# Clearing a value tile in eight pieces, and spreading one-hot tiles over more half pairs, in a chunked attention and top-1 mixture-of-experts kernel

## The chip, the cores and the metric

The kernel runs on one core of a Trainium2 chip. The metric is the device time of one execution in microseconds (us). The kernel before takes 444.6 us, the median of three runs (444.13, 444.6, 446.34).

## What is computed

Attention over chunks of 32 queries, each of which sees 8 memory rows, its own chunk, 16 rows to the left and 8 to the right; then, on the rows of all heads side by side, a mixture of 8 experts in which each token goes to the one with the largest logit.

```
for c in range(nc):                       # B, H, S, D = 4, 8, 768, 64; chunks of 32
    l_start, r_end = max(0, 32*c - 16), min(S, 32*c + 40)
    k_full = concat([mem_k, k[:, :, l_start:r_end]]); v_full likewise
    a = softmax(scale * q_c @ k_full.T)
    out[:, :, c_start:c_end] = a @ v_full
x = out as [3072, 512]
logits = x @ w_gate + modality_bias[modality_id]
e_idx = argmax(logits); gate_w = softmax(logits)[e_idx]
out[mask_e] = gate_w * (relu(x[mask_e] @ w1[e]) @ w2[e])   # 8 experts, 512 -> 1024 -> 512
```

## The kernel before

The kernel has two stages. The first does the attention and, beside it, the routing of the tokens. The second gathers the tokens of each expert from a copy of x in memory and does the two matrix products.

**The attention loop** (`for i in range(n + 2)`, line 894) goes over 16 pairs of heads, `u`, each in two half pairs, `hf`, so 32 steps `i`. Four pairs make a batch. It is a software pipeline written out by hand: TensorE (PE), SyncE (SP) and GpSimd (POOL) keep the order of the program throughout (line 50), VectorE (DVE) and ScalarE (ACT) keep it up to step 26 (`MAN`). In step `i` PE gets, in this order: `scores` of this half pair (line 351); `exps_t` of the one before, a transpose of the scores less their maximum (line 369), from which ACT makes the exponentials `PT` (line 371); in a first half (`hf == 0`) the transposes of the next pair's keys (`trans_k`, lines 333 and 337), which ACT copies into the tile `kbd` in four copies (`store_k`, line 343), and in a second half the transposes of the next pair's queries (`trans_q`, line 315), copied by ACT to `qT` (line 320); `trans_x` of the half pair two steps back (line 404); and `attend` of the one before, the weighted sum of values (line 381). DVE has, in a step, the maximum and the subtraction (`less_max`, lines 359 and 362), in a first half the regrouping of the next pair's queries to `qr` (line 306), and `normalize` of the half pair before (`den`, its reciprocal, and the product `xb`, lines 389, 391, 396). POOL shares the value rows between chunks (`share_v`, line 301, eight copies for a pair), writes the memory keys of the pair after the next into `kbd` (`mem_keys`, line 325) and issues the store of `xb` (line 409). PSUM tiles of the name `tr` (`bank()`) come from four buffers that all these transposes share.

**The value tiles.** There are three, `vws[0]` to `vws[2]`, used in turn by the pairs. Each holds two heads beside each other with zeros across, and the zeros are written once, ahead of a tile's first use: those of the third tile by two DVE memsets of 64 partitions x 24 x 64, one after `normalize` of step 1 (line 952) and one after `less_max` of step 2 (line 907). Pair 2 first needs the tile in step 5.

**The routing** of batch `b` is a generator, `route(b)` (line 536), appended when the batch's last attention rows are transposed. It yields "v" after each DVE or POOL instruction and "pe" or "late" ahead of work for PE. `pump(k)` (line 414), called all over the loop with k = 1, 3 or 5, takes up to k instructions from it. A wait for PE is taken up only by the last `pump(1, True)` of a step, behind `attend`, and only so many steps after the yield: for batches 0 and 1 one step after "pe" and two after "late", for batch 2 none and one. The parts that the change touches are, for batches 0 and 1: the logits reach DVE (line 553), DVE finds the largest (`oh`, line 572), ACT takes exponentials (`rex`, line 575), `yield "pe"` (line 576), PE forms the ranks by products with `ones_b` and `tri_b` (lines 581 to 586), DVE goes on with gate, rank, `lo` and `ac` (lines 589 to 615), then six pairs of one-hot tiles, `l1` (128 x 128, line 654) and `a1` (128 x 192, line 656), two pairs by POOL and four by DVE, then `yield "late"` and the six table products on PE (line 664).

```
def pump(k, pe=False):
    ...
        if wait:
            if not pe or now[0] < since + (wait == "late" or b < B - 2) + (wait == "late" and b < B - 2):
                return
...
eng = nc.gpsimd if t < (NPOOL, NPOOL, NPOOL, NP3)[b] else nc.vector
```

Constants for the routing (`more_constants`, line 194) are made by DVE in the same way from step 4 on.

Of the kernel before, what the change touches and what calls it, by code (L numbers as in the profile page):

```python
# [20 lines left out]
P = 128  # L21
B, H, S, D = 4, 8, 768, 64
NMEM = 8
NCH = S // 32
NT = S // P
# [28 lines left out]
def tile_chunk_attention_top1_moe(  # L54
# [14 lines left out]
    nc = tc.nc  # L69
# [24 lines left out]
    def bank():  # L94
        return ps.tile([P, 512], F32, name="tr", tag="tr", bufs=4)
# [33 lines left out]
    vws = [(sv if i == 1 else pers).tile([P, NCH, VW], F32, name=f"vw{i}", align_bytes=256) for i in range(NVW)]  # L129
# [140 lines left out]
    def edge_v(i):  # L270
        t = vws[i]
        for h in range(2):
            r = slice(64 * h, 64 * h + 64)
            nc.gpsimd.memset(t[r, :, 2 * D:2 * D + 2], 0.0)
            nc.gpsimd.memset(t[r, 1:NCH - 1, 2 * D + h:2 * D + h + 1], 1.0)
            nc.gpsimd.memset(t[r, 0:NCH:NCH - 1, h * D:h * D + D], 0.0)
            nc.gpsimd.tensor_copy(t[r, 0:NCH:NCH - 1, 2 * D + h:2 * D + h + 1], vedge[r])
# [61 lines left out]
    def store_k(u, h, j, copy):  # L339
        tt = kts[u, h][64 * j:64 * j + 64]  # L340
        win = bass.AP(tensor=tt.tensor, offset=tt.offset, ap=[list(tt.ap[0]), [16, NCH], [1, 28]])
        dst = kbds[u % 2][64 * h:64 * h + 64, :, h, 0:56]
        copy(dst.rearrange("p c (i j) -> p c i j", j=2)[:, :, :, j], win)  # L343
# [12 lines left out]
    def less_max(u, hf):  # L356
        scf = scs.pop((u, hf))[:, 0:384].rearrange("p (a m) -> p a m", m=64)
        mx = sm.tile([P, 6, 1], F32, name="mx")
        nc.vector.reduce_max(mx, scf, axis=AX.X)
        pump(1)  # L360
        sb = sbs[u, hf] = wk.tile([P, 6, 64], F32, name="sb")
        nc.vector.tensor_sub(sb, scf, mx.to_broadcast([P, 6, 64]))
# [49 lines left out]
    routing, now = [], [0]  # L412

    def pump(k, pe=False):
        k = 1 if routing and routing[0][2] < 0 else k * KB if routing and routing[0][2] == B - 2 else k
        while k > 0 and routing:
            g, wait, b, since = routing[0]
            if wait:
                if not pe or now[0] < since + (wait == "late" or b < B - 2) + (wait == "late" and b < B - 2):
                    return  # L420
                pe = False
            r = next(g, None)
            if r is None:
                routing.pop(0)
                return
            routing[0] = (g, r if r != "v" else "", b, now[0])
            k -= r == "v"


    plan = {}  # L430
# [105 lines left out]
    def route(b):  # L536
# [36 lines left out]
        yield "v"  # L573
        ex = sm.tile(sh, F32, name="rex")
        nc.scalar.activation(ex, l, AF.Exp)
        yield "pe"

        rkb = bank()
        rkf = rkb[:, 0:(NT + 1) * E]
# [60 lines left out]
        for t in range(NT):  # L640
            l1 = rt.tile([P, P], F32R, name="l1", bufs=NT)
            a1 = rt.tile([P, 192], F32R, name="a1", bufs=NT)
            T = b * NT + t
            if b == B - 1 and NP3 <= t < NP3 + NACT:
                dist = sm.tile([P, 192], F32, name="dist", bufs=2)
                nc.scalar.activation(dist[:, 0:P], iota[:, 0:P], AF.Abs, scale=-1.0, bias=lo[:, t])
                nc.scalar.activation(l1, dist[:, 0:P], AF.Relu, scale=-1.0, bias=1.0)
                dist = sm.tile([P, 192], F32, name="dist", bufs=2)
                nc.scalar.activation(dist, iota, AF.Abs, scale=-1.0, bias=ac[:, t])
                nc.scalar.activation(a1, dist, AF.Relu, scale=tokn[:, T:T + 1], bias=tokm[:, T:T + 1])  # L650
                hot.append((l1, a1))
                continue
            eng = nc.gpsimd if t < (NPOOL, NPOOL, NPOOL, NP3)[b] else nc.vector
            eng.tensor_scalar(l1, iota[:, 0:P], lo[:, t], None, op0=ALU.is_equal)
            yield "v"
            eng.tensor_scalar(a1, iota, ac[:, t], tokm[:, T:T + 1], op0=ALU.is_equal, op1=ALU.mult)
            yield "v"
            hot.append((l1, a1))
        if b == B - 1:
            plan_early()  # L660
# [210 lines left out]
    t = bank()  # L871
# [3 lines left out]
    mem_keys(0, nc.gpsimd)  # L875
    nc.gpsimd.memset(vws[1][64:P, :, 0:D], 0.0)
    edge_v(1)
    for h in (1, 0):
        for j in range(2):
            store_k(0, h, j, nc.vector.tensor_copy if j else nc.scalar.copy)  # L880
# [13 lines left out]
    for i in range(n + 2):  # L894
# [8 lines left out]
            exps_t(*units[i - 1])  # L903
        if live:
            less_max(u, hf)
            if i in (1, 2):
                nc.vector.memset(vws[i][0:64, :, D:2 * D], 0.0)
            pump(1)
        if u + 1 < NU and hf == 0:
            trans_k(u + 1)  # L910
# [37 lines left out]
            trans_x(*units[i - 2])  # L948
        if 1 <= i < n:
            normalize(*units[i - 1])  # L950
            if i == 1:
                nc.vector.memset(vws[2][64:P, :, 0:D], 0.0)
            pump(1)
        if i >= 2:
            u2, hf2 = units[i - 2]
            if hf2 == 1 and u2 % 4 == 3:
                routing.append((route(u2 // 4), True, u2 // 4, 0))
# [197 lines left out]
```

## Time and profile before

| | before |
|---|---|
| median of three runs | 444.6 us |
| the profiled execution | 441.84 us |
| its span, first to last instruction | 440.1 us |
| mean granted TensorE clock | 0.989 of full |
| busy: PE, DVE, ACT, POOL | 415.1, 309.8, 268.6, 208.2 us |

The attention loop takes about the first 138 us, the experts the rest. The profile is of one execution, which is 2.8 us under the median of the runs. A share of busy time over the span mixes the two stages, so the views by stretch and the timelines are what to read; PE's busy time holds the modelled ends of pipelined matmuls and is no proof that PE sets the pace.

### The profile page before, as it was taken

How to read it: one execution, taken by the hardware profiler on the slowest of the kernel's cores; microseconds unless marked ns; L12 is line 12 of the kernel's file. 1: busy time of each engine (PE TensorE's matmuls, PEld its weight loads, DVE VectorE, ACT ScalarE, POOL GpSimd, SP SyncE). 2: the span in 40 equal slices, each digit the busy share in tenths (PEclk: the TensorE clock that was granted, in tenths of full speed). 3: DMA queues.
4: the chain of work that ended last, by engine and by line, in shares of the span. 5: the costliest groups of instructions: out<-in, count | busy, mean ns of one | idle time of the engine just before them, and what ended most of it. 6: DMA issues, size and time to landing. Idle time of an engine off the chain costs nothing. (4 is left out here: it accounts for less than half of the span.)

```text
span 440.1 us, 11873 instructions
## 1 busy us (share of the span) xinstructions
PE 415.1 (94%) x4053; PEld 355.7 (81%) x4053; DVE 309.8 (70%) x754; ACT 268.6 (61%) x537; POOL 208.2 (47%) x407
## 2 busy tenths in 40 slices
PE   7799998999987998999999999999999999999993
PEld 4677777777765886989798998989898989898982
DVE  6898797697796999658456466776768684959530
ACT  5868786787656664647365456666666565657521
POOL 7898889999687932550053305404041215220101
PEclk9999998999998999999999999999999999999998
DMA  6969998888566301296195967505596404350101
GB/s 191 234 167 249 219 262 239 231 231 228 131 185 221 138 8 48 97 259 208 38 281 170 243 182 262 170 32 161 124 250 206 140 5 148 99 144 1 48 1 48
DMA packets 78307, 69.31 MB, mean 158 GB/s; under 512 B 36763, under 2 KB 64563, under 8 KB 78228
## 3 DMA queue, kind: packets, MB, share of 16 engines
q1 hardware_dynamic: 71488, 48.84, 40.2%
q0 software_dynamic: 5888, 19.41, 14.8%
q8 instruction: 37, 0.61, 0.6%
q14 instruction: 42, 0.34, 0.2%
q10 hardware_dynamic: 852, 0.11, 0.2%
HBM read 81.25 MB, written 16.58 MB: 222 GB/s over the span
## 5 line engine op out<-in xcount | busy, mean ns | idle before, releaser
L803 PEld LDWEIGHTS tr<-xt,w 128*128 128x128 f32 x1152 | 140.8, 188 | 5.2 <-issue 2.8
L803 PE MATMUL tr<-xt,w 128*128 128x256 f32 (+1 forms) x1152 | 142.8, 284 | 2.1 <-PEq L1116 0.8
L813 PE MATMUL av<-wh,h 128*128 128x512 f32 x384 | 125.0, 397 | 0.0
L807 DVE SCALAR_TENSOR_TENSOR h<-tr,h 128x256 fp32r<-128x256 f32 x96 | 40.5, 423 | 66.8 <-ACT h L804 42.6
L813 PEld LDWEIGHTS av<-wh,h 128*128 128x128 f32 x384 | 72.1, 188 | 16.6 <-issue 0.4
L813 PE MATMUL av<-wl,h 128*128 128x512 f32 x192 | 75.6, 394 | 0.0
L301 POOL COPY vw<-vw 24x384 f32<-24x384 f32 (+1 forms) x128 | 67.2, 525 | 9.4 <-DMA vw<-in_v_dram 3.1
L804 ACT ACTIVATE h<-tr 128x256 fp32r<-128x256 f32 x96 | 36.9, 386 | 54.4 <-PE tr L803 40.7
L728 DVE TENSOR_TENSOR wl<-raw,wh 128x512 fp32r<-128x512 f32 x91 | 64.4, 708 | 7.0 <-ACT wh L726 0.5
L838 POOL DMA_INDIRECT out_dram<-o,ix x24 | 24.7, 1027 | 93.5 <-ACT o L834 90.7
L728 DVE TENSOR_TENSOR w<-raw,w 128x512 fp32r<-128x512 f32 x93 | 60.8, 693 | 5.9 <-ACT w L726 5.9
L726 ACT CAST wh<-raw 128x512 fp32r<-128x512 f32 x96 | 58.8, 616 | 0.0
L726 ACT CAST w<-raw 128x512 fp32r<-128x512 f32 x96 | 52.9, 623 | 0.0
L343 ACT COPY kbd<-tr 64x672 f32<-64x672 f32 x62 | 48.3, 778 | 5.4 <-DMA raw<-in_moe_modality_id_dram 2.2
L813 PEld LDWEIGHTS av<-wl,h 128*128 128x128 f32 x192 | 36.1, 188 | 7.6
L834 ACT ACTIVATE o<-av,gate 128x512 f32<-128x512 f32 x24 | 16.2, 689 | 39.2 <-PE av L813 27.3
L746 POOL DMA_INDIRECT xg<-xd,gx x24 | 26.7, 1111 | 17.0 <-POOL gx L744 5.5
L371 ACT ACTIVATE PT<-tr 128x384 f32<-128x384 f32 x32 | 15.8, 494 | 26.3 <-PE tr L369 26.1
L381 PE MATMUL av<-vw,PT 128*32 128x130 f32 x768 | 28.8, 284 | 2.7 <-ACT PT L371 2.7
L351 PE MATMUL sc<-kbd,qT 128*32 128x128 f32 x768 | 28.3, 279 | 1.3 <-DVE kbd L343 1.3
L381 PEld LDWEIGHTS av<-vw,PT 128*32 128x32 f32 x768 | 19.8, 111 | 8.2 <-issue 4.1
L351 PEld LDWEIGHTS sc<-kbd,qT 128*32 128x32 f32 x768 | 21.0, 112 | 5.0 <-issue 3.5
(251 smaller groups left out, 515.2 us busy)
## 6 DMA issues: line engine op xcount, KB each, us to landing
raw<-in_moe_w_dram SPq DMA_DIRECT2D x192, 256.0 KB
k<-in_k_dram SPq DMA_DIRECT2D x16, 384.0 KB
q<-in_q_dram SPq DMA_DIRECT2D x16, 384.0 KB
xd<-xb POOLq DMA_DIRECT2D x16, 384.0 KB, 4.8
vw<-in_v_dram SPq DMA_DIRECT2D x32, 184.0 KB
xs<-xg SPq DMA_DIRECT2D x14, 256.0 KB
xq<-xs SPq DMA_DIRECT2D x28, 128.0 KB
vw<-in_mem_v_dram SPq DMA_DIRECT2D x32, 48.0 KB
```

Source lines behind the costliest of these rows:

```text
L301: nc.gpsimd.tensor_copy(vw[r0:r0 + 24, c + 1:c + 1 + w, d], vw[r0 + 32:r0 + 56, c:c + w, d])
L343: copy(dst.rearrange("p c (i j) -> p c i j", j=2)[:, :, :, j], win)
L351: nc.tensor.matmul(sc[32 * j:32 * j + 32, t * P:(t + 1) * P], qT[:, 32 * c:32 * c + 32], kbd[:, c].rearrange("p h m -> p (h m)"), start=Tr ...
L381: nc.tensor.matmul(avb[32 * j:32 * j + 32, t * W:(t + 1) * W], PT[:, t * P + 32 * j:t * P + 32 * j + 32], vw[:, c, 0:W], start=True, stop= ...
L726: nc.scalar.copy(wh[i], raw[i])
L728: (eng or nc.vector).tensor_sub(wl[i][:, s], raw[i][:, s], wh[i][:, s].bitcast(F32))
L746: nc.gpsimd.indirect_dma_start(out=xg[t], out_offset=None, in_=xd[0:rows], in_offset=bass.IndirectOffsetOnAxis(ap=gx[:, t:t + 1], axis=0))
L803: nc.tensor.matmul(pw, wt[i][:, j * P:(j + 1) * P], x[:, c, 0:w], start=(n == 0), stop=(n == 11))
L804: nc.scalar.activation(hh[:, f], ph, AF.Relu)
L807: nc.vector.scalar_tensor_tensor(hl[:, f], ph, 0.0, hh[:, f].bitcast(F32), op0=ALU.max, op1=ALU.subtract)
L813: nc.tensor.matmul(pos[t], x, w[8 + f], start=(f == 0 and n == 0), stop=(f == 7 and n == 2))
L838: nc.gpsimd.indirect_dma_start(out=out, out_offset=bass.IndirectOffsetOnAxis(ap=to[:, t:t + 1], axis=0), in_=outs[t], in_offset=None, boun ...
```

## The change

It does two things. The two large memsets of the third value tile become eight of 64 partitions x 6 x 64 (`clear_v`): three after `normalize` of step 2, three after that of step 3, two after `less_max` of step 4. And the routing of batches 0 and 1 is paced in another way: the rank products wait for nothing but the last `pump(1, True)` of the same step ("now"); a DVE one-hot instruction yields "h", which counts 3 where k is 3 and 1.6 elsewhere, and is not begun with less than 1.5 left, so that a step gets fewer of them; the table products wait one step after the last tile in place of two.

```diff
--- before.py
+++ after.py
@@ -413,10 +413,14 @@
 
     def pump(k, pe=False):
         k = 1 if routing and routing[0][2] < 0 else k * KB if routing and routing[0][2] == B - 2 else k
+        heavy = 3 if k == 3 else 1.6
         while k > 0 and routing:
             g, wait, b, since = routing[0]
-            if wait:
-                if not pe or now[0] < since + (wait == "late" or b < B - 2) + (wait == "late" and b < B - 2):
+            if wait == "h":
+                if k < 1.5:
+                    return
+            elif wait:
+                if not pe or now[0] < since + (wait == "late" or wait != "now" and b < B - 2):
                     return
                 pe = False
             r = next(g, None)
@@ -424,7 +428,7 @@
                 routing.pop(0)
                 return
             routing[0] = (g, r if r != "v" else "", b, now[0])
-            k -= r == "v"
+            k -= heavy if r == "h" else r == "v"
 
 
     plan = {}
@@ -573,7 +577,7 @@
         yield "v"
         ex = sm.tile(sh, F32, name="rex")
         nc.scalar.activation(ex, l, AF.Exp)
-        yield "pe"
+        yield "now" if b < B - 2 else "pe"
 
         rkb = bank()
         rkf = rkb[:, 0:(NT + 1) * E]
@@ -651,10 +655,11 @@
                 hot.append((l1, a1))
                 continue
             eng = nc.gpsimd if t < (NPOOL, NPOOL, NPOOL, NP3)[b] else nc.vector
+            slow = "h" if b < B - 2 and eng is nc.vector else "v"
             eng.tensor_scalar(l1, iota[:, 0:P], lo[:, t], None, op0=ALU.is_equal)
-            yield "v"
+            yield slow
             eng.tensor_scalar(a1, iota, ac[:, t], tokm[:, T:T + 1], op0=ALU.is_equal, op1=ALU.mult)
-            yield "v"
+            yield slow if t < NT - 1 else "v"
             hot.append((l1, a1))
         if b == B - 1:
             plan_early()
@@ -875,6 +880,12 @@
     mem_keys(0, nc.gpsimd)
     nc.gpsimd.memset(vws[1][64:P, :, 0:D], 0.0)
     edge_v(1)
+    clears = [vws[2][64 * h:64 * h + 64, c:c + 6, (1 - h) * D:(2 - h) * D] for c in range(0, NCH, 6) for h in range(2)]
+
+    def clear_v(k):
+        for _ in range(k):
+            nc.vector.memset(clears.pop(0), 0.0)
+
     for h in (1, 0):
         for j in range(2):
             store_k(0, h, j, nc.vector.tensor_copy if j else nc.scalar.copy)
@@ -903,8 +914,10 @@
             exps_t(*units[i - 1])
         if live:
             less_max(u, hf)
-            if i in (1, 2):
-                nc.vector.memset(vws[i][0:64, :, D:2 * D], 0.0)
+            if i == 1:
+                nc.vector.memset(vws[1][0:64, :, D:2 * D], 0.0)
+            if i == 4:
+                clear_v(2)
             pump(1)
         if u + 1 < NU and hf == 0:
             trans_k(u + 1)
@@ -948,8 +961,8 @@
             trans_x(*units[i - 2])
         if 1 <= i < n:
             normalize(*units[i - 1])
-            if i == 1:
-                nc.vector.memset(vws[2][64:P, :, 0:D], 0.0)
+            if i in (2, 3):
+                clear_v(3)
             pump(1)
         if i >= 2:
             u2, hf2 = units[i - 2]
```

How that moves the instructions is shown at three places.

**DVE at step 4, ahead of pair 3's queries.** `vw_128` is the third value tile, `q_281` the queries of pair 3, `iota`, `rev`, `base` and `ones_b` are constants. Before:

```order
L396 TENSOR_TENSOR xb<-av,den 128x384
L195 CAST iota<-raw 128x192
L674 COPY base<-iota 64x8
L359 TENSOR_REDUCE mx<-sc 128x6
L197 TENSOR_SCALAR rev<-iota 128x8
L362 TENSOR_TENSOR sb<-sc,mx 128x384
L199 MEMSET ones_b 128x128
L306 COPY qr<-q_281 128x2x6x64
```

Now:

```order
L396 TENSOR_TENSOR xb<-av,den 128x384
L887 MEMSET vw_128 64x6x64 x3
L195 CAST iota<-raw 128x192
L359 TENSOR_REDUCE mx<-sc 128x6
L197 TENSOR_SCALAR rev<-iota 128x8
L679 COPY base<-iota 64x8
L362 TENSOR_TENSOR sb<-sc,mx 128x384
L887 MEMSET vw_128 64x6x64 x2
L199 MEMSET ones_b 128x128
L306 COPY qr<-q_281 128x2x6x64
```

Three pieces stand behind the `xb` of step 3 and two more ahead of the `qr` of pair 3; three others stand behind the `xb` of step 2. The two large memsets stood ahead of the `qr` of pair 2, earlier than this piece.

**PE where batch 0's ranks are formed.** The piece begins in the second half of pair 5; `kbd_124` belongs to pair 6. Before:

```order
L404 MATMUL tr<-ident,xb 128x128 x3
L381 MATMUL av<-vw_128,PT 32x130 x12
L351 MATMUL sc<-kbd_124,qT 32x128 x12
L369 MATMUL tr<-ident,sb 128x128 x3
L333 MATMUL tr<-ident,k_919 128x128 x3
L337 MATMUL tr<-ident,mkp 128x2x8
L333 MATMUL tr<-ident,k_919 128x128 x3
L337 MATMUL tr<-ident,mkp 128x2x8
L404 MATMUL tr<-ident,xb 128x128 x3
L381 MATMUL av<-vw_128,PT 32x130 x12
L581 LDWEIGHTS ones_b
L581 MATMUL tr<-tot,ones_b 128x56
```

Now, to where the rank products begin (the scores of pair 6 follow behind the last of them, with `tri_b`):

```order
L315 MATMUL tr<-ident,qr 128x128 x6
L404 MATMUL tr<-ident,xb 128x128 x3
L381 MATMUL av<-vw_128,PT 32x130 x12
L585 LDWEIGHTS ones_b
L585 MATMUL tr<-tot,ones_b 128x56
L587 LDWEIGHTS ones_b
L587 MATMUL tr<-oh,ones_b 128x48
```

The rank products stood behind the weighted sum of the following first half; they now stand behind that of the second half, ahead of pair 6's scores. Batch 1 moves in the same way. The table products keep their place behind the same weighted sum as before.

**DVE at batch 0's one-hot tiles.** Before, from `less_max` of a first half:

```order
L362 TENSOR_TENSOR sb<-sc,mx 128x384
L306 COPY qr<-q_1079 128x2x6x64
L654 TENSOR_SCALAR l_1389<-iota,lo 128x128
L656 TENSOR_SCALAR a_1390<-iota,ac,tokm 128x192
L654 TENSOR_SCALAR l_1393<-iota,lo 128x128
L656 TENSOR_SCALAR a_1394<-iota,ac,tokm 128x192
L654 TENSOR_SCALAR l_1401<-iota,lo 128x128
L656 TENSOR_SCALAR a_1402<-iota,ac,tokm 128x192
L389 TENSOR_SCALAR den<-av 128x6
L654 TENSOR_SCALAR l_1426<-iota,lo 128x128
L391 RECIPROCAL den<-den 128x6
L656 TENSOR_SCALAR a_1427<-iota,ac,tokm 128x192
```

Now, from `less_max` of the second half ahead of it:

```order
L362 TENSOR_TENSOR sb<-sc,mx 128x384
L659 TENSOR_SCALAR l_1315<-iota,lo 128x128
L661 TENSOR_SCALAR a_1316<-iota,ac,tokm 128x192
L659 TENSOR_SCALAR l_1340<-iota,lo 128x128
L661 TENSOR_SCALAR a_1341<-iota,ac,tokm 128x192
L389 TENSOR_SCALAR den<-av 128x6
L391 RECIPROCAL den<-den 128x6
L396 TENSOR_TENSOR xb<-av,den 128x384
L359 TENSOR_REDUCE mx<-sc 128x6
L362 TENSOR_TENSOR sb<-sc,mx 128x384
L306 COPY qr<-q_1085 128x2x6x64
L659 TENSOR_SCALAR l_1403<-iota,lo 128x128
```

All eight instructions stood ahead of the next `xb`; now four stand ahead of it, two behind the next `qr`, and the last two in the half pair after. On DVE `oh` itself keeps its place. On POOL the gate's store and the four one-hot instructions of each of the two batches now stand ahead of one more `share_v` and `mem_keys`.

## Rows read from the trace of the kernel before

**Rows 1.** Stretches: start:end, length, PE, PEld, DVE, ACT, POOL busy, clock, DMA share, GB/s
```profile
20.00:30.00 10.00, 8.18 (x142) 6.46 (x135) 9.06 (x27) 7.59 (x14) 9.21 (x16) 1.00 0.78 197
...
60.00:70.00 10.00, 8.37 (x155) 6.85 (x158) 8.82 (x27) 6.71 (x13) 9.07 (x15) 0.92 0.92 243
```

**Rows 2.** The chain that ended last, earliest long piece: start, length, what
```profile
364.63 11.67 PE tr L803 x96
```

**Rows 3.** Timeline of PE, pairs 3 to 5: start, length, line, count, idle before
```profile
31.14 0.86 PE L351 MATMUL sc<-kbd,qT 128*32 128x128 f32 x24
...
38.13 0.86 PE L351 MATMUL sc<-kbd,qT 128*32 128x128 f32 x24
...
43.30 0.87 PE L315 MATMUL tr<-ident,qr 128*128 128x128 f32 x6 [0.24 <-ACT kbd L343]
```

**Rows 4.** Timeline of DVE, 3 to 30 us: clears, and the copy of q
```profile
3.07 1.34 DVE L135 MEMSET vw<- 64x1536 f32 x1 [0.27 <-issue]
...
4.68 1.34 DVE L136 MEMSET kbd<- 64x1536 f32 x1 [0.27 <-issue]
...
27.29 0.50 DVE L306 COPY qr<-q 128x768 f32<-128x768 f32 x1
...
29.23 0.55 DVE L396 TENSOR_TENSOR xb<-av,den 128x384 f32<-128x384 f32 x1
```

**Rows 5.** Timeline of PE, 22 to 30 us
```profile
22.15 0.84 PE L315 MATMUL tr<-ident,qr 128*128 128x128 f32 x6 [1.49 <-DVE den L389]
...
29.92 0.52 PE L404 MATMUL tr<-ident,xb 128*128 128x128 f32 x3
```

**Rows 6.** Timeline of POOL, 30 us
```profile
30.34 0.74 POOL L325 COPY kbd<-memT 64x192 f32<-64x192 f32 x2
```

**Rows 7.** Timeline of PE around the routing of batch 0
```profile
53.00 0.87 PE L381 MATMUL av<-vw,PT 128*32 128x130 f32 x24
...
53.69 0.84 PE L351 MATMUL sc<-kbd,qT 128*32 128x128 f32 x24
...
57.58 0.20 PE L581 MATMUL tr<-tot,ones_b 128*128 128x56 bf16 x1
...
57.88 0.86 PE L351 MATMUL sc<-kbd,qT 128*32 128x128 f32 x24
...
68.12 0.58 PE L404 MATMUL tr<-ident,xb 128*128 128x128 f32 x3 [1.40 <-DVE xb L396]
...
68.62 1.53 PE L381 MATMUL av<-vw,PT 128*32 128x130 f32 x24
...
69.92 1.51 PE L351 MATMUL sc<-kbd,qT 128*32 128x128 f32 x24
...
79.27 0.84 PE L351 MATMUL sc<-kbd,qT 128*32 128x128 f32 x24
```

**Rows 8.** Timeline of DVE around the routing of batch 0
```profile
55.08 0.15 DVE L389 TENSOR_SCALAR den<-av 128x6 f32<-128x6 f32 x1
...
55.20 0.29 DVE L572 TENSOR_TENSOR oh<-rev,me 128x48 bf16<-128x48 f32 x1
...
67.42 0.55 DVE L396 TENSOR_TENSOR xb<-av,den 128x384 f32<-128x384 f32 x1
```

**Rows 9.** Timeline of PE around the routing of batch 1
```profile
86.59 0.84 PE L351 MATMUL sc<-kbd,qT 128*32 128x128 f32 x24
...
101.21 0.86 PE L351 MATMUL sc<-kbd,qT 128*32 128x128 f32 x24
...
109.69 0.84 PE L351 MATMUL sc<-kbd,qT 128*32 128x128 f32 x24
```

**Rows 10.** Timeline of DVE at the routing of batch 1
```profile
87.43 0.21 DVE L572 TENSOR_TENSOR oh<-rev,me 128x48 bf16<-128x48 f32 x1
```

**Rows 11.** Timeline of POOL from batch 0's one-hot tiles to pair 9's memory keys
```profile
66.90 0.75 POOL L654 TENSOR_SCALAR l<-iota,lo 128x128 fp32r<-128x128 f32 x1
...
74.83 0.74 POOL L325 COPY kbd<-memT 64x192 f32<-64x192 f32 x2
```

## The prediction

> **What bounds the kernel now.** I read the stretches of ten us first. They show where engines run short: from 20 to 30 us and from 60 to 70 us DVE and POOL are each busy for about nine us of ten, and in the second stretch the granted clock of TensorE is 0.92, in the first 1.00 [rows 1]. The chain of waits comes next; its first long piece begins at 364.63 us, so it says nothing of the attention loop [rows 2]. What the loop loses is carried whole to the experts, since their first products wait for the routing; I count a loss or gain in the loop one to one in the end. So the timelines of the loop decide.
>
> Undisturbed, a pair takes 6.99 us from scores to scores (31.14 to 38.13 us), and the query transposes in its second half stand behind ACT's key copies (the 0.24 us wait at 43.30 us) [rows 3]. That is a loop through two engines: query transposes, transposes of half pair outputs, weighted sum, scores and transposed scores on PE; exponentials and four key copies on ACT; query transposes again. What PE waits for between the query transposes of a second half and the next scores is lost in full; in a first half, behind the key transposes, PE has time to spare while ACT copies. Three places stand out. At 22.15 us PE has waited 1.49 us: the queries' copy stood behind the second memset of the third value tile [rows 5]. At 68.12 us it has waited 1.40 us for an `xb` that DVE began at 67.42, behind eight one-hot instructions, and after that the clock was low: the weighted sum took 1.53 us where 0.87 is usual, the scores 1.51 where 0.84 is [rows 7, 8]. Batch 1 has the same instructions and no such wait: from the scores of pair 10 to those of pair 13 it is 109.69 - 86.59 = 23.10 us [rows 9], where batch 0, pair 6 to pair 9, takes 79.27 - 53.69 = 25.58 [rows 7]. So 2.48 us is what batch 0's crowd of one-hot tiles costs.
>
> **Term 1, the memsets.** Two memsets in a row start 1.61 us apart (3.07 and 4.68), though each row shows 1.34 [rows 4]. So the two of the third tile cost 3.2 us. A piece is a quarter: 0.40 us if the 0.27 us gap belongs to the work, 1.34 / 4 + 0.27 = 0.61 if each instruction pays it. I take 0.43, near the first, as a gap that is the same in front of a kbd and a vw tile of one size looks like work that the row leaves out; eight pieces make 3.4 us (3.2 to 4.9). The wait at 22.15 us goes, but nothing is kept of it: POOL's memory keys for pair 3, which the change leaves alone, end at 30.34 + 0.74 = 31.08 [rows 6], and pair 3's scores already start at 31.14 [rows 3]. So the gain is at most 0.06. The other way is open. All eight pieces still stand ahead of pair 3's `qr`, DVE does the same work plus 0.2 us, and it now comes early to weighted sums that are not there yet, where a memset filled the time before. I put that idling at 0.3 us (between 0 and the 1.49 us by which PE's old wait moves). `qr` (27.29) and the `xb` at 29.23 move back by 0.5 us, PE's transposes at 29.92 follow that `xb` at once [rows 4, 5], and so does everything behind. Term 1: +0.5 us, from -0.06 to 1.7 + 0.3 = +2.0.
>
> [...]
>
> **Term 2, batch 0.** What goes: the crowd, 2.48 us. What comes: the rank products now stand directly behind a second half's weighted sum, at 53.69 us in the trace's time, ahead of pair 6's scores, and all but the first read `oh`. DVE's order up to `oh` is unchanged, and there `oh` runs from 55.20 to 55.49 [rows 8]. PE waits, then needs about 0.3 us for the products (57.58 to 57.88 where they stood) [rows 7]; pair 6's scores start at 55.82 and not 53.69, 2.13 us later. They stand in the part of the loop where nothing hides a wait; their old place, in a first half, cost little. Behind this DVE has caught up, and the one-hot instructions are four, two and two. I replay: 55.82, a pair of 6.99, 0.25 for an `xb` that comes late behind `lo` and `ac` (an estimate, below the 1.40 us of the old wait), a pair of 6.99, and for the pair with the table products and the next logits 109.69 - 101.21 = 8.48 [rows 9]. Pair 9's scores start at 78.53, before at 79.27. Term 2: -0.7 us. Its ends: -2.5 if `oh` were there in time, +1.4 if the 2.13 us came and the crowd's cost stayed but for the slow clock (0.66 + 0.67 us by the two long rows).
>
> **Term 3, batch 1.** Here PE is at the place at 86.59 us [rows 9] and `oh` ends at 87.64 [rows 10]; with 0.05 us to be seen by PE and the products' 0.3, pair 10's scores come 1.4 us later. Two pairs of 6.99 and one of 8.48 then make 1.4 + 22.46 = 23.86 us against 23.10. Term 3: +0.8 us, from 0 (`oh` in time) to +1.4.
>
> **What costs nothing.** The table products do not move on PE, so neither does the next batch's start. On POOL the gate's store and one-hot tiles go ahead of one `share_v` and `mem_keys` more. From the first one-hot to the end of the memory keys behind a `share_v` POOL needs 74.83 + 0.74 - 66.90 = 8.67 us [rows 11]; it can start when `ac` and `lo` are there, some 5 us after `oh` (estimate), at 60.5, and end at 69.2. Pair 8's scores, which need those keys, are due at 53.69 + 2.13 + 14.23 = 70.05. That covers it by 0.9 us; without the cover it is a wait on the critical loop.
>
> **Sum:** 0.5 - 0.7 + 0.8 = +0.6 us. The profiled execution, 441.84 us with a span of 440.1, would become 442.4; it lies 2.8 us under the median of the runs, and I carry the difference over: 444.6 + 0.6 = **445.2 us**, no change that can be told. (0.5%, 2.2 us, is about what can.)
>
> **Rivals.**
> - *The ranks find `oh` ready.* If DVE is less behind, `oh` ends as early as it can: the weighted sum ends at 53.87, `den` begins, and from there to the end of `oh` it is 0.41 us (55.08 to 55.49) [rows 7, 8], so 54.28 in place of 55.49: 1.2 us less in batch 0, 0.5 in batch 1 by the same distance from PE's place, and the memsets' 0.5 may go too: 445.2 - 2.2 = 443.0. In addition the timed runs, 2.8 us over the profiled one, may hold a second crowd at batch 1; the change would then take out up to 2.5 more: 440.5. For it: DVE's rows before `oh` are long in batch 0. Against: nothing on DVE ahead of `oh` is removed. I put it at 442.0.
> - *The clock falls behind the new waits.* This ends slower. The new wait in batch 0, from 53.87 to 55.5 us, is longer than the 1.40 us one after which the rows show the long weighted sum and scores, 1.3 us in excess; the one in batch 1 is about 0.9. Each fall costs 1.3: 446.5 with one, 447.8 with both. It decides when a wait of some 1.4 us is enough. For it: the wait at 66.7 us, and the 0.92 in that stretch. Against: 1.49 us at 20.7 left the clock at 1.00 [rows 1, 5]. [...]
> - *POOL comes late.* If its one-hot tiles start 2 us later than I reckon, pair 8's scores wait 1.1 us: 446.3. The margin is thin, but the start hangs on DVE alone.
>
> **How the numbers follow.** Forecast 0.44, ranks ready 0.22, clock 0.28 (one fall 0.18, both 0.10), POOL 0.06. Faster by over 0.5%, under 442.4: most of the first rival, 0.18. Slower, over 446.8: both falls, half of one fall with a full term 1, and a little of the rest, 0.23. Within: 0.59. The range leaves out the far halves of both rivals: 442.3 to 447.8.
>
> **What would show it.** Right: no wait for `xb` near 68 us, no low clock there; PE idle for 1 to 2 us in front of the rank products of batch 0 and about 1 us in batch 1, released by `oh`; pair 3's scores no earlier than 31.1 us, with PE waiting for `qr` or `xb` between 27 and 31 us; pair 9's scores within 1 us of 79.3 and pair 13's within 1.5 us of 109.7. Wrong: rank products that start at once behind the weighted sum; pair 13's scores under 107.5 or over 112; or a loop that ends earlier while the experts do not.

## The result, and the profile after

The changed kernel takes 444.41 us (median of 21 runs), the kernel before, run beside it on the same chip, 441.94 (21 runs). The ratio is 1.0059, 95% interval 1.0033 to 1.0084: slower by 2.6 us (1.5 to 3.7). The three runs of before that stand at the head of this document (444.6) were high; nearly all of the closeness of the forecast, 445.2, to 444.41 is the luck of that. Each run below is compared with before on its own chip. The profiles of e2_route and e8_cut are of slow executions, which the ratios leave out; of the first only the times are used, of the second one DVE row too.

| | after |
|---|---|
| profiled execution, span | 444.37, 442.6 us |
| mean granted clock | 0.988 |
| busy: PE, DVE, ACT, POOL | 415.3, 312.9, 268.9, 206.3 us |

The stretches of the changed kernel, as in [rows 1]: start and end, length, busy time of PE, PEld, DVE, ACT and POOL, granted clock, DMA share, GB/s.

```profile
20.00:30.00 10.00, 7.89 (x133) 6.11 (x132) 8.92 (x28) 8.07 (x16) 7.82 (x17) 1.00 0.94 247
60.00:70.00 10.00, 9.56 (x172) 7.32 (x166) 9.19 (x28) 8.64 (x17) 8.99 (x15) 1.00 0.78 194
```

From 60 to 70 us PE is now busy for 9.56 us in place of 8.37, at a clock of 1.00 in place of 0.92. What came instead stands in the timeline of PE, at the places of [rows 3, 5, 7, 9], with the scores behind batch 2's table products last:

```profile
28.67 0.84 PE L315 MATMUL tr<-ident,qr 128*128 128x128 f32 x6 [1.04 <-ACT PT L371]
...
30.56 0.52 PE L404 MATMUL tr<-ident,xb 128*128 128x128 f32 x3 [1.05 <-DVE xb L396]
...
31.70 0.84 PE L351 MATMUL sc<-kbd,qT 128*32 128x128 f32 x24
...
55.76 0.29 PE L587 MATMUL tr<-oh,ones_b 128*128 128x48 bf16 x6 [1.28 <-DVE oh L576]
...
56.03 0.86 PE L351 MATMUL sc<-kbd,qT 128*32 128x128 f32 x24
...
68.66 0.55 PE L404 MATMUL tr<-ident,xb 128*128 128x128 f32 x3
...
69.96 0.86 PE L351 MATMUL sc<-kbd,qT 128*32 128x128 f32 x24
...
78.44 0.84 PE L351 MATMUL sc<-kbd,qT 128*32 128x128 f32 x24
...
87.23 0.29 PE L587 MATMUL tr<-oh,ones_b 128*128 128x48 bf16 x6 [1.15 <-DVE oh L576]
...
87.49 0.86 PE L351 MATMUL sc<-kbd,qT 128*32 128x128 f32 x24
...
109.92 0.84 PE L351 MATMUL sc<-kbd,qT 128*32 128x128 f32 x24
...
130.24 1.51 PE L351 MATMUL sc<-kbd,qT 128*32 128x128 f32 x24
```

The rank products (L587) wait 1.28 us in batch 0 and 1.15 in batch 1, each released by `oh`, and the scores stand right behind them. The transposes of half pair outputs (L404) at 68.66 us wait for nothing, where [rows 7] had 1.40 us and a low clock (0.50 granted from 68.60 to 71.50 us in that profile). Ahead of pair 3's scores there are two new waits of a microsecond (28.67, 30.56). DVE there, the clears and the copy behind them:

```profile
20.32 1.37 DVE L887 MEMSET vw<- 64x384 f32 x3
...
23.91 1.37 DVE L887 MEMSET vw<- 64x384 f32 x3
...
27.00 0.88 DVE L887 MEMSET vw<- 64x384 f32 x2
...
28.02 0.50 DVE L306 COPY qr<-q 128x768 f32<-128x768 f32 x1
```

`qr` starts at 28.02, in [rows 4] at 27.29; counted from pair 0's scores, which start at 9.72 here and at 9.98 before, it is 0.99 us later. Behind the clears the next instructions start at 21.62, 25.31 and 27.94, so a piece costs 0.43 to 0.47 us.

Where the time went is read best from the starts of the scores (L351) in each timeline of PE. Each column is the time from one such start to another: pair 0 to pair 3 (clears), 3 to 6 (rank products of batch 0 at the end), 6 to 9 (its tiles and tables), 9 to 10 (rank products of batch 1 at the end), 10 to 13, pair 13 to the second half of 14, from there to pair 15 (batch 2's table products at the end, "tables"), then to the experts' first product; "path" is from pair 0 to pair 15. The second row is the kernel before, profiled again (e5_before).

| profile of | 0-3 | 3-6 | 6-9 | 9-10 | 10-13 | 13-14 | tables | path | to experts |
|---|---|---|---|---|---|---|---|---|---|
| before, first | 21.16 | 22.55 | 25.58 | 7.32 | 23.10 | 11.86 | 6.26 | 117.83 | 12.36 |
| before, second | 21.18 | 22.48 | 23.82 | 7.28 | 23.26 | 11.84 | 7.62 | 117.48 | 14.75 |
| after | 21.98 | 24.33 | 22.41 | 9.05 | 22.43 | 12.33 | 7.99 | 120.52 | 12.05 |
| e1_clears | 22.67 | 22.98 | 23.40 | 7.29 | 22.67 | 12.28 | 7.73 | 119.02 | 11.66 |
| e3_spread | 21.15 | 22.52 | 23.10 | 7.29 | 22.62 | 12.56 | 7.93 | 117.17 | 11.40 |
| e4_ranks | 21.19 | 24.47 | 22.45 | 8.95 | 22.43 | 12.33 | 7.82 | 119.64 | 11.66 |
| e6_mid | 21.20 | 22.53 | 23.33 | 7.28 | 23.57 | 12.48 | 7.89 | 118.28 | 11.68 |
| e12_mid2 | 21.18 | 22.55 | 23.49 | 7.29 | 23.37 | 12.48 | 7.89 | 118.25 | 14.76 |
| e7_share | 21.15 | 22.53 | 23.77 | 7.28 | 23.28 | 11.84 | 8.46 | 118.31 | 12.81 |
| e9_three | 21.15 | 22.53 | 24.07 | 7.28 | 23.29 | 12.08 | 6.24 | 116.64 | 12.28 |
| e10_change3 | 22.05 | 24.97 | 22.43 | 9.05 | 22.44 | 12.33 | 6.02 | 119.29 | 12.29 |
| e11_spread3 | 21.20 | 22.58 | 22.65 | 7.31 | 22.66 | 12.35 | 6.03 | 114.78 | 11.89 |

Against the second profile of before the change's path is 3.04 us longer: +0.80 at the clears, +1.85 and +1.77 at the two places of the rank products, -1.41 and -0.83 in the stretches behind them, +0.49 and +0.37 around batch 2's tables. The timed difference is +2.6. The last column is not in this sum: there the second profile of before lies 2.70 us above after, so that up to the experts' first product the two are only 0.34 us apart, and after and the first profile of before 2.38. A stretch of over 14 us to the experts stands in two of the twelve profiles, e5_before and e12_mid2, and is a matter of the execution (see e12_mid2 below). So the columns say where the change loses; one pair of executions does not add up to the timed difference.

### The profile page after: what moved, and what is told of

It reads as the page before. It is cut to its first block, busy times and chain, and to the rows that moved or that the text cites. A ratio compares the mean times of both kernels' runs of the same rounds, so it can differ in the third digit from the quotient of the medians.

```text
span 442.6 us, 11876 instructions
## 1 busy us (share of the span) xinstructions
PE 415.3 (94%) x4053; PEld 355.2 (80%) x4053; DVE 312.9 (71%) x760; ACT 268.9 (61%) x537; POOL 206.3 (47%) x407
## 5 line engine op out<-in xcount | busy, mean ns | idle before, releaser
L301 POOL COPY vw<-vw 24x384 f32<-24x384 f32 (+1 forms) x128 | 64.8, 507 | 9.9 <-DMA vw<-in_v_dram 3.4
L733 DVE TENSOR_TENSOR wl<-raw,wh 128x512 fp32r<-128x512 f32 x91 | 63.3, 695 | 8.4 <-ACT wh L731 1.3
L351 PE MATMUL sc<-kbd,qT 128*32 128x128 f32 x768 | 28.6, 284 | 1.3 <-DVE kbd L343 1.3
L381 PE MATMUL av<-vw,PT 128*32 128x130 f32 x768 | 28.2, 281 | 1.5 <-ACT PT L371 1.5
L351 PEld LDWEIGHTS sc<-kbd,qT 128*32 128x32 f32 x768 | 21.0, 113 | 5.6 <-issue 4.5
L381 PEld LDWEIGHTS av<-vw,PT 128*32 128x32 f32 x768 | 19.7, 111 | 6.9 <-issue 3.8
```

Of the source, the lines that this page charges most:

```text
L301: nc.gpsimd.tensor_copy(vw[r0:r0 + 24, c + 1:c + 1 + w, d], vw[r0 + 32:r0 + 56, c:c + w, d])
L351: nc.tensor.matmul(sc[32 * j:32 * j + 32, t * P:(t + 1) * P], qT[:, 32 * c:32 * c + 32], kbd[:, c].rearrange("p h m -> p (h m)"), start=Tr ...
L381: nc.tensor.matmul(avb[32 * j:32 * j + 32, t * W:(t + 1) * W], PT[:, t * P + 32 * j:t * P + 32 * j + 32], vw[:, c, 0:W], start=True, stop= ...
L733: (eng or nc.vector).tensor_sub(wl[i][:, s], raw[i][:, s], wh[i][:, s].bitcast(F32))
```

## The experiments

**First four: the parts of the change, each by itself.** e1_clears is the kernel before with the eight clears only:

```
-            if i in (1, 2):
-                nc.vector.memset(vws[i][0:64, :, D:2 * D], 0.0)
+            if i == 1:
+                nc.vector.memset(vws[1][0:64, :, D:2 * D], 0.0)
+            if i == 4:
+                clear_v(2)
...
-            if i == 1:
-                nc.vector.memset(vws[2][64:P, :, 0:D], 0.0)
+            if i in (2, 3):
+                clear_v(3)
```

Expected: 

> Only the eight clears, the routing as before. Theory A (the ranks' wait in the critical half pair is what costs): +0.5 us against the kernel before, pair 3's scores about 0.5 us later. Theory B (batch 2's one-hot tiles on VectorE meet GpSimd's value copies, and how they meet is a matter of their offset): 0 or +2.4 us as the offset falls, with the six table products of batch 2 taking 2.6 us or 4.2 us. Theory C (the clears are the main cost): +2 us, with pair 3's scores 0.5 us later and a low clock behind it.

Measured: 442.91 us, ratio 1.005 (1.0025 to 1.0075), +2.2 us. This is more than the +0.5 that Theory A gave it, and near Theory C's +2 with a low clock behind pair 3's scores. PE in its profile, up to pair 3's scores:

```profile
29.85 0.87 PE L404 MATMUL tr<-ident,xb 128*128 128x128 f32 x3 [0.78 <-DVE xb L396]
30.66 1.53 PE L381 MATMUL av<-vw,PT 128*32 128x130 f32 x24
31.96 1.29 PE L351 MATMUL sc<-kbd,qT 128*32 128x128 f32 x24
```

The same waits as in the changed kernel, and behind them, by the length of the products, the low clock: a weighted sum (L381) of 1.53 us where 0.87 is usual, as in the first profile of before at the granted 0.50. Pair 0 to pair 3 takes 1.5 us longer than before, without such a fall (the changed kernel) 0.8. e10_change3 has the fall as well, the sums at 30.87 and the scores at 32.08 us; so it is one execution's chance, in two of three profiles with the clears moved.

e2_route is the changed kernel with the two old memsets: all of the routing, none of the clears. Expected: 

> Only the routing's new pacing (ranks sooner, one-hot tiles spread), the clears as before. Theory A: +2 us, rank products waiting 1.2 us or more for the one-hot expert choice in batches 0 and 1. Theory B: 0 or +2.4 us by the offset at batch 2. Theory C: +0.5 us.

Measured: 444.15 us, ratio 1.0093 (1.0055 to 1.0131), +4.1 us, more than any of the theories gave. The routing is slower by itself; the parts do not add up to the whole in the times (2.2 and 4.1 against 2.6), within intervals of 1 to 2 us each.

e3_spread has only the spread, with rank and table products at their old places:

```
-            k -= r == "v"
+            k -= heavy if r == "h" else r == "v"
...
+            slow = "h" if b < B - 2 and eng is nc.vector else "v"
...
-            yield "v"
+            yield slow
```

(`heavy` is 1.5 for k = 3, else 1, so that four one-hot instructions go into each of two half pairs.) Expected: 

> Only the spreading: ranks and table products where they were before, the eight VectorE one-hot instructions of batches 0 and 1 as four and four in two half pairs, the clears as before. Theory A: 1.2 us faster than before (0 to 2.5), and no wait of PE for the attention rows behind batch 0's one-hot tiles. Theory B: -1.2 or +1.2 us by the offset at batch 2. Theory C: the same as before.

Measured: 440.79 us, ratio 1.0009 (0.9978 to 1.004): the 1.2 us of Theory A did not come, and a wait for `xb` is left behind batch 0's tiles:

```profile
67.29 0.52 PE L404 MATMUL tr<-ident,xb 128*128 128x128 f32 x3 [0.48 <-DVE xb L396]
```

In the loop the spread gives 0.72 us in batch 0 and 0.64 in batch 1 against the second profile of before, but 0.72 is lost from pair 13 to 14 and 0.31 at the tables: the path is 0.3 us shorter, which the times cannot tell.

e4_ranks has only the rank products a half pair sooner; crowd and table products stay:

```
-        yield "pe"
+        yield "now" if b < B - 2 else "pe"
...
-                if not pe or now[0] < since + (wait == "late" or b < B - 2) + (wait == "late" and b < B - 2):
+                if not pe or now[0] < since + (wait == "late") + 2 * (wait == "late" and b < B - 2):
```

Expected: 

> Only the ranks half a pair sooner in batches 0 and 1, the one-hot tiles in a crowd of six and two as before (also half a pair sooner), the table products in their old place, the clears as before. Theory A: +3 us: the wait in front of the ranks in both batches (about 1.3 us each, and 0.3 us of products), and no gain from the spreading. Theory B: 0 or +2.4 us by the offset. Theory C: the same as before.

Measured: 443.88 us, ratio 1.0065 (1.0034 to 1.0096), +2.9 us, as Theory A says. Its waits:

```profile
55.33 0.29 PE L587 MATMUL tr<-oh,ones_b 128*128 128x48 bf16 x6 [1.35 <-DVE oh L576]
...
65.14 0.52 PE L404 MATMUL tr<-ident,xb 128*128 128x128 f32 x3 [0.27 <-DVE xb L396]
...
86.72 0.29 PE L587 MATMUL tr<-oh,ones_b 128*128 128x48 bf16 x6 [1.08 <-DVE oh L576]
```

3-6 and 9-10 are 1.99 and 1.67 us longer than before; 6-9 and 10-13 are 1.37 and 0.83 shorter, nearly the same as in the changed kernel (22.41, 22.43), though the one-hot tiles are still six and two. So in this profile the wait for `xb` is shorter even without the spread: it is 0.27 us in batch 0 here and 0.48 in e3_spread, against 1.2 to 1.4 in the profiles of before, e7_share and e9_three. Both edits take most of the same wait away, and only this one pays for it. Net of what the stretches behind give back, the early rank products cost 0.62 us of path in batch 0 and 0.84 in batch 1.

**What was odd in the first profile.** e5_before is the kernel before, unchanged. Expected: 

> The kernel before, unchanged, profiled a second time, because its first profile disagrees with those of the other kernels in two places. In the first profile batch 0 (scores of pair 6 to scores of pair 9) took 25.58 us, while e1_clears, which issues the same routing instructions in the same order, took 23.40; and the last stretch with batch 2's tables (second scores of pair 14 to scores of pair 15) took 6.26 us, in every other profile 7.7 to 8.0. Theory A (both were peculiarities of one execution, which hid each other): batch 0 near 23.1 and the tables near 7.8 here. Theory B (the first profile was typical, and the offset that the edits bring changes both places): 25.6 and 6.3 again.

Measured: 442.8 us (one execution). Batch 0 took 23.82, the tables 7.62: Theory A, though not all the way in batch 0. PE at the places of [rows 7], and at the tables:

```profile
67.08 0.52 PE L404 MATMUL tr<-ident,xb 128*128 128x128 f32 x3 [1.29 <-DVE xb L396]
67.53 0.87 PE L381 MATMUL av<-vw,PT 128*32 128x130 f32 x24
68.22 0.84 PE L351 MATMUL sc<-kbd,qT 128*32 128x128 f32 x24
...
124.27 0.36 PE L664 MATMUL tr<-a,l 128*128 128x192 f32 x1 [0.75 <-DVE a L656]
125.36 0.36 PE L664 MATMUL tr<-a,l 128*128 128x192 f32 x1 [0.73 <-DVE a L656]
126.40 0.35 PE L664 MATMUL tr<-a,l 128*128 128x192 f32 x1 [0.68 <-DVE a L656]
126.68 1.09 PE L351 MATMUL sc<-kbd,qT 128*32 128x128 f32 x24
...
129.18 1.51 PE L351 MATMUL sc<-kbd,qT 128*32 128x128 f32 x24
```

The wait for `xb` behind the crowd is there again (1.29 us), the low clock behind it is not: of the 2.48 us of the first profile the fall was the part that does not come every time. At batch 2 the table products now wait three times for DVE's tiles, and there the clock falls (0.76 granted from 127 to 134 us, where the first profile had 1.00). DVE and POOL at that place:

```profile
122.52 0.58 DVE L656 TENSOR_SCALAR a<-iota,ac,tokm 128x192 fp32r<-128x192 f32 x1
123.03 0.60 DVE L654 TENSOR_SCALAR l<-iota,lo 128x128 fp32r<-128x128 f32 x1
123.55 0.66 DVE L656 TENSOR_SCALAR a<-iota,ac,tokm 128x192 fp32r<-128x192 f32 x1
...
122.50 4.22 POOL L301 COPY vw<-vw 24x384 f32<-24x384 f32 x8
```

And the same in the first profile of before:

```profile
125.31 0.27 DVE L654 TENSOR_SCALAR l<-iota,lo 128x128 fp32r<-128x128 f32 x1
125.50 0.37 DVE L656 TENSOR_SCALAR a<-iota,ac,tokm 128x192 fp32r<-128x192 f32 x1
...
124.99 5.55 POOL L301 COPY vw<-vw 24x384 f32<-24x384 f32 x8
```

One kernel, two executions: once the first six of DVE's eight one-hot instructions keep their 0.27 to 0.37 us and POOL's eight copies take 5.55, once the copies take 4.22 and all but the first of the eight 0.58 to 0.67. In each of the two profiles one side or the other takes longer; why, and what decides which, no run shows.

**Is it the place or the earliness?** e6_mid takes e4_ranks and issues the rank products one place later, behind the next pair's scores:

```
+            elif wait == "now":
+                if pe or now[0] <= since:
+                    return
```

Expected: 

> Only the rank products of batches 0 and 1 come sooner, but one place behind where the change puts them: behind the next pair's scores and transposed scores, in a first half, ahead of the key transposes. VectorE's chain up to the one-hot tiles comes forward nearly as in the change; the clears, the crowd of six and two one-hot instructions and the table products stay as before. Theory A (what costs is that the wait for oh stands ahead of the scores of a second half's end, where nothing hides it): the wait goes, since oh ends before the scores and transposed scores are through; pair 6 to pair 9 about 22.6 us, pair 9 to pair 10 7.3 us, as in e3_spread, and the time within 1 us of before, against +3 us for e4_ranks. Theory B (an earlier VectorE chain costs by itself, whatever PE waits for): +2 to +3 us like e4_ranks.

Measured: 443.8 us, ratio 1.0046 (1.0011 to 1.0081), +2.0 us; its profile:

```profile
55.04 0.29 PE L590 MATMUL tr<-oh,ones_b 128*128 128x48 bf16 x6
...
60.36 0.52 PE L404 MATMUL tr<-ident,xb 128*128 128x128 f32 x3 [0.67 <-DVE xb L396]
...
64.04 0.52 PE L404 MATMUL tr<-ident,xb 128*128 128x128 f32 x3 [0.26 <-DVE xb L396]
...
85.92 0.29 PE L590 MATMUL tr<-oh,ones_b 128*128 128x48 bf16 x6 [0.32 <-DVE oh L579]
```

The waits of 1.35 and 1.08 us are gone or down to 0.32, and 3-6 and 9-10 are back at 22.53 and 7.28. So much for Theory A: the wait hangs on the place, and 3-6 and 9-10 are longer by 1.7 to 2.0 us with it. But part of that comes back behind it: 6-9 and 10-13 are 23.33 and 23.57 us here, 22.45 and 22.43 in e4_ranks, with two waits for `xb` in batch 0 (0.67 and 0.26 us) in place of one of 0.27. Over both stretches the place is worth 1.06 us in batch 0 and 0.53 in batch 1. And the time did not come back to before: +2.0 is what Theory B gave, and within the intervals it is not told apart from the +2.9 of e4_ranks. Since its profiled execution was the fastest of twelve, the same kernel was profiled again as e12_mid2. Expected: 

> e6_mid once more, for a second profile: its first showed 439.5 us at a clock of 0.997, the fastest of its twelve runs, and a loop as long as that of before, while the median of its runs was 0.5% over before. Theory A (the profiled execution was a lucky one; rank products in a first half wait too, or lower the clock, in others): pair 6 to pair 9 or pair 10 to pair 13 some 0.5 to 1.5 us longer than the 23.33 and 23.57 of its first profile. Theory B (the loss lies behind the loop, in the tables of batch 2): the loop as in its first profile and a longer stretch from pair 14 to the experts' first products.

Measured: 444.48 us. The loop agrees with the first profile within 0.2 us in every column; the stretch to the experts is 14.76 in place of 11.68 us. By stretches (columns as above), e6_mid:

```profile
127.00:134.00 7.00, 4.11 (x83) 3.03 (x83) 4.72 (x13) 1.35 (x3) 4.43 (x8) 1.00 1.04 286
134.00:141.00 7.00, 5.18 (x72) 3.95 (x73) 5.32 (x12) 5.60 (x12) 4.40 (x8) 1.00 0.35 108
```

and e12_mid2:

```profile
127.00:134.00 7.00, 5.68 (x83) 4.20 (x83) 3.72 (x10) 1.30 (x3) 4.45 (x8) 0.76 1.04 277
134.00:141.00 7.00, 4.96 (x57) 3.30 (x58) 4.02 (x11) 3.19 (x7) 3.24 (x6) 0.62 0.08 29
```

As Theory B says, the loss lies behind the loop. The three table waits are the same in both profiles (0.75, 0.73 to 0.74 and 0.69 us), and the clock holds behind them in e6_mid and falls in e12_mid2. That fall by itself is not the 3.1 us: the profile of after has it too (1.51 us for the scores at 130.24), and so have those of e1_clears, e3_spread, e4_ranks and e7_share, and they reach the experts in 11.40 to 12.81 us. PE behind the tables, e6_mid:

```profile
134.40 0.55 PE L404 MATMUL tr<-ident,xb 128*128 128x128 f32 x3 [2.61 <-DVE xb L396]
...
139.87 3.53 PE L811 MATMUL tr<-xt,w 128*128 128x256 f32 x24 [0.70 <-ACT xt L769]
```

and e12_mid2:

```profile
130.58 1.51 PE L351 MATMUL sc<-kbd,qT 128*32 128x128 f32 x24
...
135.40 0.70 PE L404 MATMUL tr<-ident,xb 128*128 128x128 f32 x3 [2.03 <-DVE xb L396]
136.03 1.53 PE L381 MATMUL av<-vw,PT 128*32 128x130 f32 x24
...
142.97 3.45 PE L811 MATMUL tr<-xt,w 128*128 128x256 f32 x24
```

In e12_mid2 the `xb` comes 1.0 us later, and behind the wait for it the clock falls a second time; from there to the experts it takes 7.57 us in place of 5.47, which is the other 2.1. e5_before has both falls as well (0.76 and 0.51 granted in the same two stretches), and 14.75 us. Of the +2.0 us in the times the path shows 0.8; that the rest is a more frequent fall is possible, not shown.

**Batch 2's tiles.** e7_share issues the copies of pair 15's value rows a half pair sooner (`share_v(u + 1)` for pair 15 behind `regroup_q` of the first half). Expected: 

> The kernel before, but GpSimd's copies of the shared value rows of pair 15 are issued half a pair earlier, so that they no longer run beside VectorE's one-hot tiles of batch 2. Theory A (the two engines slow each other there: in the changed kernel's profile VectorE's tiles took 0.58 to 0.67 us beside copies of 4.22 us for eight, in the first profile of before 0.27 and 0.37 beside copies of 5.55): the second scores of pair 14 to the scores of pair 15 take about 6.3 us in place of 7.8, and the time is 1 to 1.5 us below before. Theory B (the tiles are late for another reason, the chain of ranks ahead of them): 7.8 us again and no change of the time.

Measured: 444.29 us, ratio 1.006 (1.0031 to 1.0089), +2.7 us. Neither theory's figure came. Six of DVE's eight one-hot instructions ran at 0.27 to 0.37 us again, but POOL made its own tiles only behind the copies: the table products waited 1.11 us for POOL's, and PE 1.04 us for an `xb`. The tables took 8.46 us. The collision was moved, not removed: of the small DVE instructions beside the moved copies `hi` took 0.47 us and `noth` 0.47, in e5_before, ahead of the copies, 0.16 and 0.21.

e8_cut cuts the third tile's two clears into four pieces each at their old places. Expected: 

> The kernel before, but the two clears of the third value tile are each cut into four, at their old places (e1_clears cuts and moves them). Theory A (the cut is nearly free, 8 pieces of 0.47 against 3.2 us, and it is the move towards pair 3 that costs): pair 0 to pair 3 within 0.4 us of 21.16, the time within 0.6 us of before. Theory B (pieces cost by their number): pair 0 to pair 3 about 0.8 us longer, as in the changed kernel, and +1 to +2 us in the time, as in e1_clears.

Measured: 442.41 us, ratio 0.9994 (0.9962 to 1.0026). Four pieces:

```profile
17.36 1.60 DVE L956 MEMSET vw<- 64x384 f32 x4
```

That is 0.40 us a piece, the 1.61 us of one whole memset [rows 4] divided by four. The cut is free; it is the move towards pair 3 that costs.

e9_three lets POOL make three of batch 2's six pairs of tiles, ahead of its copies:

```
-            eng = nc.gpsimd if t < (NPOOL, NPOOL, NPOOL, NP3)[b] else nc.vector
+            eng = nc.gpsimd if t < (NPOOL, NPOOL, 3, NP3)[b] else nc.vector
```

Expected: 

> The kernel before, but GpSimd makes three of batch 2's six pairs of one-hot tiles in place of two, ahead of its copies of pair 15's value rows, and VectorE three in place of four. GpSimd's copies then start some 1.6 us later (0.6 and 1.0 us a pair of tiles, e5_before), behind VectorE's tiles. Theory A (in the last stretch VectorE's tiles are held up by GpSimd's copies: in e5_before tiles of 0.58 to 0.67 us, three waits of 0.7 us of the table products, and a low clock behind them): tiles of 0.27 and 0.37 us, second scores of pair 14 to scores of pair 15 about 6 us in place of 7.6, no long scores behind it, the time 1.5 to 3 us below before. Theory B (the tables wait for GpSimd's own tiles then): a wait released by GpSimd of about 1 us, as in e7_share, and no gain.

Measured: 439.97 us, ratio 0.9957 (0.9928 to 0.9986), 1.9 us faster than before. Its rows:

```profile
124.24 0.42 DVE L656 TENSOR_SCALAR a<-iota,ac,tokm 128x192 fp32r<-128x192 f32 x1
124.59 0.30 DVE L654 TENSOR_SCALAR l<-iota,lo 128x128 fp32r<-128x128 f32 x1
...
126.12 0.69 PE L664 MATMUL tr<-a,l 128*128 128x192 f32 x4 [1.30 <-POOL a L656]
126.74 0.86 PE L351 MATMUL sc<-kbd,qT 128*32 128x128 f32 x24
```

Both theories hold a part: the tiles are short, the tables wait 1.30 us for POOL's third, and the stretch is still 1.4 us shorter, with scores at full clock behind it (1.00 granted from 127 to 134 us).

e10_change3 is the whole change with the same line. Expected: 

> The whole change, with three of batch 2's pairs of one-hot tiles on GpSimd as in e9_three. Theory A (what the change loses, it loses in pairs 2, 6 and 10 and not at batch 2): 2.0 to 3.0 us slower than e9_three, as the change is against before. Theory B (a good part of its loss is that it meets GpSimd's copies at a worse offset): within 1 us of e9_three.

Measured: 444.14 us, ratio 1.004 (1.0011 to 1.0069). Against e9_three that is 1.004 / 0.9957 = 1.0083, 3.7 us. So the change's loss is not a matter of how it meets batch 2 (Theory A). Whether 3.7 is more than the 2.6 us it loses against before, the intervals do not tell.

e11_spread3 is e3_spread with the same line. Expected: 

> e3_spread (the one-hot instructions of batches 0 and 1 as four and four, rank and table products where they were) with three of batch 2's pairs of tiles on GpSimd. By the sum of its parts: batch 0 near 23.1 us in every execution and the gain of e9_three, so the same as e9_three or up to 0.5 us better; if the crowd of six and two is a common loss in timed runs, 1 us better or more.

Measured: 439.92 us, ratio 0.9932 (0.9901 to 0.9963): 3.0 us faster than before, with no wait for `xb` in either batch and the shortest path of all profiles, 114.78 us. It has the spread without the early rank products, the clears where they were, three pairs of tiles on POOL. Whether the spread adds to e9_three is not shown: the path is 1.9 us shorter, but the profiled execution here was the second fastest of twelve and that of e9_three the third slowest, and in the times the intervals overlap.

## Why the prediction was right and wrong

The forecast was 445.2 us in a range of 442.3 to 447.8, no change the likeliest; 444.41 lies in the range, and the change is slower by 0.59%, just outside what was called no change. The mechanism was right in terms 1 and 3 and in what comes in term 2; the balance, +0.6 forecast and +2.6 measured, was 2 us off, and the high start made up for it by luck.

- **Term 1, the memsets: right.** "+0.5, from -0.06 to +2.0": +0.80 us in the profile of after, with `qr` 0.99 us later from pair 0's scores and PE waiting ahead of the transposes, as said. The cut costs nothing at the old places (e8_cut: 0.40 us a piece, the lower bound); in the changed kernel a piece costs 0.43 to 0.47, near the 0.43 taken. The upper bound, a gap of 0.27 us with each piece, does not show: four take 1.60 us, one whole 1.61. The size that was missed is the clock: two of three profiles with the moved clears show a fall there (products of 1.29 to 1.53 us), which adds 0.6 us or more (22.67 against 21.98 in 0-3, 24.97 against 24.33 in 3-6).
- **Term 2, batch 0: the step that failed.** "What goes: the crowd, 2.48 us." What comes was sized well: 2.13 us forecast, 1.85 measured (e4_ranks: 1.99). The replay from there was close too: 22.71 us for pairs 6 to 9, measured 22.41. But 25.58 us, from which it was subtracted, was one execution's: 23.82 in the second profile and 23.40, 23.77 and 24.07 in e1_clears, e7_share and e9_three, which have the same instructions there. So 1.41 us went, and term 2 is +0.44 in place of -0.7. The sign that 1.33 of the 2.48 us was a clock fall stood in the prediction's own row of long products; it used that in a bound, not in the forecast. The bound itself, +1.4, does not follow from its numbers: 2.13 less 1.33 is +0.8.
- **Term 3, batch 1: right, with two errors that mostly cancel.** "+0.8": the wait cost 1.77 us, not 1.4 (the 0.05 us from the end of `oh` to the products is what after shows in both batches, 55.71 to 55.76 and 87.18 to 87.23), and the stretch behind it became 0.83 us shorter, which the replay put at 0.6 (22.46 against 23.10). The sum is +0.94.
- **"What costs nothing": wrong for batch 2.** +0.86 us from pair 13 to pair 15, where the change edits nothing. The first profile of before held a lucky 6.26 us for the tables; every profile with two of the pairs on POOL but that one has 7.6 to 8.5. Two oddities of one execution, +1.8 in batch 0 and -1.4 at the tables, hid each other, and its total of 441.84 near the median of 21 runs gave no warning.
- **The anchor.** "It lies 2.8 us under the median of the runs, and I carry the difference over" took three runs as the typical time; with 21 runs the profiled execution lies at the median. Without that step the same sum would have given 442.4.
- **The rivals.** `oh` was not ready (waits of 1.28 and 1.15 us). POOL came in time: `ac` ended 4.85 us behind `oh` (60.56 and 55.71 us), near the 5 that were taken, and the scores of pair 8 at 69.96 us have no wait. The clock did not fall behind the new waits for `oh` in the profiles of after, e4_ranks and e10_change3 (in after 1.00 granted from 55 to 58 and from 86 to 90 us); it fell behind the moved clears and behind batch 2's tables, places the rival had not named. A wait of 1.30 us (e9_three) left the clock up (1.00 granted from 120 to 134 us), and three of 0.7 us brought it down in e12_mid2 (0.76 from 127 to 134 us) and not in e6_mid (1.00), the same kernel.

What stays open: why e6_mid is 2.0 us slower in the times with a path only 0.8 us longer, and with it how much of e4_ranks' +2.9 us is the place of the rank products and how much the earlier chain; and what decides whether the clock falls behind a given wait.

## What to carry to other kernels

Profile the kernel before twice before subtracting anything: a stall that is followed by a low clock can be partly chance (batch 0 took 25.58 and 23.82 us in two executions of one kernel), and a total near the median can hide two opposite oddities. In a hand-written pipeline ask in which half a product that waits would stand: moved from a first half, behind the key transposes, to the end of a second, ahead of the scores, the same rank products made the stretch with them 1.7 to 2.0 us longer each time, and 0.6 to 0.8 us were left of it behind the next three pairs. When small VectorE instructions share a stretch with GpSimd copies, moving a tile to the slower engine, ahead of its copies, can help: 1.9 us in e9_three, though a pair of tiles takes POOL 1.59 to 1.64 us in the first profile of before and DVE 0.63 to 0.64.

## What was not expected of the hardware

- Which of DVE and POOL gives way in a shared stretch changes between executions of one kernel: 5.55 us for POOL's eight copies and 0.27 to 0.37 us for six of DVE's eight instructions (the first profile of before), or 4.22 and 0.58 to 0.67 for seven of them (e5_before).
- A DVE memset of 1536 elements per partition shows 1.34 us and takes 1.61 [rows 4]; four of 384 in a row take 1.60 (e8_cut). So the 0.27 us that the row leaves out did not come back with each instruction.
- With the same three waits of 0.7 us ahead, the stretch from pair 15's scores to the experts' first product takes 11.68 or 14.76 us in two executions of one kernel, at clocks of 1.00 and 1.00, or 0.76 and 0.62 (127 to 134 and 134 to 141 us). The fall behind the tables is not enough for it: five profiles that have this one, and not the second behind the `xb`, take 11.40 to 12.81 us.
